# Local attention's weighted sums added up by accumulating DMAs, and a second fold on GpSimd, in a gated mix of two attentions

## Chip, core and metric

One core of a Trainium2 chip runs the kernel in one launch. The metric is the device time of one execution in microseconds (us); lower is better. TensorE is called PE below, VectorE DVE, ScalarE ACT, GpSimd Pool, and SyncE, which issues most DMAs, SP.

## What is computed

The input x has 2048 rows of 448 numbers. Two attention blocks of 16 heads of 28 numbers read it, and a gate mixes their results:

```
g = sigmoid((x * gate_w).sum(-1))
a = local attention A: q, k, v = x @ wqkv;  row s sees rows s, s-2, ..., s-14 (8 offsets w, step 2)
      logits[s, w] = q[s] . k[s - 2w] * 28**-0.5;  softmax over w;  o[s] = sum over w of p[s, w] * v[s - 2w];  o @ wo
b = full attention B: every row sees all 2048 rows;  o @ wo
out = g * a + (1 - g) * b
```

Everything is float32; products that need the precision are split into a high and a low part and summed from three matmuls.

## The kernel before

The kernel has three stages. Until about 254 us PE projects x to q, k and v of both blocks. From there until about 829 us it computes the full attention B, and beside it the local attention A, which uses no PE at all. From there to the end it multiplies both results by the output weights.

**The middle stage** has 256 steps: 16 units (four groups of heads by four blocks of 512 columns) of 16 steps each. A step is one pass of the loop `for kt in range(NJ)`. In it PE makes the scores of four heads (line 960), three matmuls of an early pass that looks for the maximum scores of a later unit (line 142), and the weighted sum of the step before (line 926). ACT takes the exponentials (line 965, two of 128x1024 per step), DVE the maxima (line 148). When a unit's maxima are complete, `max_parts` reduces them (line 176), ACT negates them, Pool makes their low part (line 183), DVE transposes them (line 188), and SP stores them to DRAM (`nm`, line 193) and loads them again as two more rows of the queries (`QH<-nm`). PE's first scores of the next unit wait for that load.

**The local attention** is cut into 8 chunks c of two heads each. Rows lie over 128 partitions, 16 rows to a partition, so that one tile is 128x896 (16 rows, 56 numbers). For each chunk and each offset w:

- `a_score`: Pool multiplies q by the shifted k (line 604, 128x896), and folds the 28 products of a head to 14 by adding one half to the other (line 609, 128x448).
- `a_reduce`: DVE sums what is left to one logit per row and head (line 614). `NR[c, w]` says in how many pieces, and `a_score` folds `3 - NR` times: with 2 once, with 1 twice.
- `a_softmax`: nine small steps on Pool, DVE and ACT (lines 616 to 644).
- `a_av`: Pool multiplies v by the weight of this offset (line 654, part 0), into `oat` for w = 0 and into a tile `prod2` for the others, and then adds `prod2` to `oat` (line 659, part 1). `prod2` and the products of `a_score` share one tag of five buffers.

After the last addition of a chunk SP stores `oat` to DRAM (`oa_scr`, line 662). When all chunks are done, `a_done` frees their buffers and sets the loads for the last stage (`op_load_b`, `op_load_a`).

**Order.** Every engine runs its instructions in the order in which the program issues them, and a waiting instruction holds up all behind it on its engine. For the local attention that order comes from a planner at build time: `item` enters each piece with a key, a cost in us and the pieces it needs, each with a lag in steps; `issue` puts a piece into the running step if its needs were issued early enough and the cost still fits (for Pool up to 4.2 us of backlog, worn down by 2.1 or 2.2 us per step). The costs are constants in the code; at run time the engines follow the order that came out of them, and the semaphores.

Of the kernel before, what the change touches and what calls it, by code (L numbers as in the profile page):

```python
# [11 lines left out]
ALU = mybir.AluOpType  # L12
# [13 lines left out]
def gated_mix_kernel(ctx: ExitStack, tc: tile.TileContext, xT, xn, gw, wA, wB, woAB, out):  # L26
    nc = tc.nc
# [180 lines left out]
    with tc.tile_pool(name="xp", bufs=1) as xp, tc.tile_pool(name="wp", bufs=2) as wp:  # L208
# [208 lines left out]
        for kt in range(3):  # L417
            if kt < 2:
                nc.vector.tensor_copy(xh[0][:, kt, :], r[:, kt, :])
            nc.vector.tensor_tensor(out=xl[0][:, kt, :], in0=r[:, kt, :], in1=xh[0][:, kt, :].bitcast(F32),  # L420
                                    op=ALU.subtract)
        nc.vector.tensor_tensor(out=tail[64:128], in0=t[64:128], in1=tail[64:128].bitcast(F32), op=ALU.subtract)
        nc.vector.tensor_tensor(out=wl0[:, 3, 0:256], in0=wt0[:, 0:256], in1=wh0[:, 3, 0:256].bitcast(F32),
                                op=ALU.subtract)
# [27 lines left out]
        for n, t in enumerate(tiles):  # L452
# [48 lines left out]
            if n == 64:  # L501
                gate = []
                for sgn, dst in ((-1.0, g_t), (1.0, omg)):
                    e = sp.tile([128, NJ], F32, name="ez")
# [14 lines left out]
    def at(pos, st, f):  # L519
        hooks.setdefault((st, pos), []).append(f)  # L520
# [10 lines left out]
    pool = ctx.enter_context(tc.tile_pool(name="psv", bufs=1, space=bass.MemoryType.PSUM))  # L531
# [56 lines left out]
    qt, Lt, oat, lst, prods = {}, {}, {}, {}, {}  # L588

    def a_load(c, nme):  # L590
        if nme == "q":
            qt[c] = a2.tile([128, NJ, 56], F32, name="qt")
            nc.sync.dma_start(qt[c], a_own[0][c])
        else:
            t = kvt[nme, c % 2]
            i = 1 if nme == "k" else 2
            nc.sync.dma_start(t[:, 0:HALO, :], a_prev[i][c, :, NJ - HALO:NJ, :])
            nc.sync.dma_start(t[:, HALO:, :], a_own[i][c])

    def a_score(c, w):  # L600
        if w == 0:
            Lt[c] = a2.tile([128, W, NJ, 2], F32, name="L", bufs=3)
        p = a3.tile([128, NJ, 56], F32, tag="prod", name="prod")
        nc.gpsimd.tensor_tensor(out=p, in0=qt[c], in1=kvt["k", c % 2][:, HALO - DIL * w:HALO - DIL * w + NJ, :],  # L604
                                op=ALU.mult)
        prods[c, w] = p.rearrange("p j (h d) -> p (j h) d", d=DH)
        for n in (DH // 2, DH // 4)[:3 - NR[c, w]]:
            lo, hi = prods[c, w][:, :, 0:n], prods[c, w][:, :, n:2 * n]
            nc.gpsimd.tensor_tensor(out=lo, in0=lo, in1=hi, op=ALU.add)  # L609
            prods[c, w] = lo  # L610

    def a_reduce(c, w, i, n):
        r = slice(2 * NJ // n * i, 2 * NJ // n * (i + 1))
        nc.vector.tensor_reduce(Lt[c][:, w].rearrange("p j h -> p (j h)")[:, r], prods[c, w][:, r], axis=X, op=ALU.add)

    def a_softmax(c, i):
        L = Lt[c].rearrange("p w j h -> p w (j h)")
        Lw = Lt[c].rearrange("p w j h -> p (j h) w")
        if i == 0:
            nc.gpsimd.tensor_tensor(out=L, in0=L, in1=maskt.rearrange("p w j h -> p w (j h)"), op=ALU.add)  # L620
        elif i in (1, 2):
            if i == 1:
                lst["m"] = a2.tile([128, NJ * 2], F32, name="lm")
            r = slice(NJ * (i - 1), NJ * i)
            nc.vector.tensor_reduce(lst["m"][:, r], Lw[:, r], axis=X, op=ALU.max)
        elif i == 3:
            nc.gpsimd.tensor_tensor(out=L, in0=L, in1=lst["m"][:, None, :].to_broadcast([128, W, NJ * 2]),
                                    op=ALU.subtract)
        elif i == 4:
            nc.scalar.activation(L, L, AF.Exp, scale=SCALE)  # L630
        elif i in (5, 6):
            if i == 5:
                lst["z"] = a2.tile([128, NJ * 2], F32, name="ls")
            r = slice(NJ * (i - 5), NJ * (i - 4))
            nc.vector.tensor_reduce(lst["z"][:, r], Lw[:, r], axis=X, op=ALU.add)
        elif i == 7:
            r = a2.tile([128, NJ, 2], F32, name="lr")
            nc.vector.reciprocal(r.rearrange("p j h -> p (j h)"), lst["z"])
            lst["r"] = r
        else:  # L640
            r = lst["r"]
            nc.gpsimd.tensor_tensor(out=r, in0=r, in1=g_t[:, :, None].to_broadcast([128, NJ, 2]), op=ALU.mult)
            nc.gpsimd.tensor_tensor(out=L, in0=L, in1=r.rearrange("p j h -> p (j h)")[:, None, :].to_broadcast(
                [128, W, NJ * 2]), op=ALU.mult)

    def a_av(c, w, part):
        if part == 0:
            if w == 0:
                oat[c] = a2.tile([128, NJ, 56], F32, name="oat")
                dst = oat[c]  # L650
            else:
                dst = a3.tile([128, NJ, 56], F32, tag="prod", name="prod2")
            oat[c, w] = dst
            nc.gpsimd.tensor_tensor(  # L654
                out=dst.rearrange("p j (h d) -> p j h d", d=DH),
                in0=kvt["v", c % 2][:, HALO - DIL * w:HALO - DIL * w + NJ, :].rearrange("p j (h d) -> p j h d", d=DH),
                in1=Lt[c][:, w, :, :, None].to_broadcast([128, NJ, 2, DH]), op=ALU.mult)
        else:
            nc.gpsimd.tensor_tensor(out=oat[c], in0=oat[c], in1=oat[c, w], op=ALU.add)  # L659
            if w == W - 1:  # L660
                stored[0] = now[0] + 4
                at("end", stored[0], lambda: nc.sync.dma_start(oa_scr[:, :, 56 * c:56 * c + 56], oat[c]))


# [3 lines left out]
    now = [0]  # L668
    stored = [0]

    def item(eng, key, name, cost, needs, f):
        lists[eng].append((key, name, cost, needs, f))

    CH, NR = 21, {}
    for c in range(8):
        for w in range(W):
            NR[c, w] = 2
    last = lambda c, w: ("r", c, w, NR[c, w] - 1)
    for c in range(8):
        c0 = CH * c - 5 * (c == 7)  # L680
        for nme in "qkv":
            item("sp", c0 if nme != "v" else c0 + 18, ("ld", nme, c), 0,
                 [(("s", c - 2, 7), 3)] if nme != "v" else [(("a", c - 2, 7, 1), 3)],
                 lambda c=c, nme=nme: a_load(c, nme))
        for w, o in enumerate((0, 2, 5, 8, 11, 14, 17, 20)):
            back = (c, w - 4) if w > 3 else (c - 1, w + 4)
            item("pool", c0 + o, ("s", c, w), 3.15 + 0.5 * (NR[c, w] == 1),
                 [(("ld", "k", c), 4), (("ld", "q", c), 4), (("a", c - 3, 7, 0), 0), (("s", c, w - 1), 0)]
                 + ([(last(*back), 0)] if back in NR else []), lambda c=c, w=w: a_score(c, w))
            for i in range(NR[c, w]):  # L690
                item("dve", c0 + o + 2 + 0.1 * i, ("r", c, w, i), 0.32,
                     [(("s", c, w), 3), (("r", c, w, i - 1) if i else last(c, w - 1) if w else ("r",), 0)],
                     lambda c=c, w=w, i=i: a_reduce(c, w, i, NR[c, w]))
        for i, (eng, o, cost, lag) in enumerate((("pool", 22, 0.68, 2), ("dve", 23, 0.35, 3), ("dve", 23.5, 0.35, 0),
                                                 ("pool", 25, 0.68, 1), ("act", 26, 0.3, 3), ("dve", 27, 0.35, 1),
                                                 ("dve", 27.5, 0.35, 0), ("dve", 27.8, 0.36, 0),
                                                 ("pool", 28, 0.9, 1))):
            item(eng, c0 + o, ("m", c, i), cost, [(last(c, 7) if i == 0 else ("m", c, i - 1), lag)],
                 lambda c=c, i=i: a_softmax(c, i))
        n = 0  # L700
        for w in range(W):
            for part in ((0,) if w == 0 else (0, 1)):
                item("pool", CH * c + 30 + 1.4 * n, ("a", c, w, part), 1.65 if part == 0 else 2.05,
                     [(("m", c, 8), 0), (("ld", "v", c), 4),
                      (("a", c, w - 1, 1 if w > 1 else 0) if part == 0 else ("a", c, w, 0), 0)],
                     lambda c=c, w=w, part=part: a_av(c, w, part))
                n += 1
    for q in lists.values():
# [350 lines left out]
```

## Time and profile before

| | before |
|---|---|
| median of 3 runs | 911.59 us (911.21 to 912.66) |
| the profiled execution | 911.58 us, span of its instructions 909.8 us |
| TensorE clock granted | 1.0 throughout |
| PE busy | 901.1 us, 99% of the span |
| DVE, ACT, Pool busy | 731.8, 649.3, 640.0 us |
| DMA | 105.06 MB, 115 GB/s on average |

The profile comes from one execution. Its 1.78 us beside the span are the start and the end around the first and last instruction. Matmuls overlap, so that PE's share says little of how near it is to its limit. `L659` in a row is line 659 of the kernel before.

### The profile page before, as it was taken

To read this page: it belongs to the slowest core of one execution; us is meant where nothing else is said; L and a number is where in the kernel's file an instruction comes from. 1 tells how busy PE (TensorE), PEld (TensorE's weight loads), DVE (VectorE), ACT (ScalarE), POOL (GpSimd) and SP (SyncE) were. 2 spreads that over 40 slices of the span, in tenths; PEclk is the share of its full clock that TensorE was granted. 3 is DMA by queue.
4 is the path that set the end of the run, shared out by engine and by line. 5 is a ranking of instruction groups with operands and counts; after the bars stand their busy time and mean duration, and the time that the engine had idled before them with its cause. 6 is when DMAs were issued, how large, how long until landed. Compare 5 with 4: busy or idle time off the path is not lost.

```text
span 909.8 us, 20654 instructions
## 1 busy us (share of the span) xinstructions
PE 901.1 (99%) x8390; PEld 547.1 (60%) x8390; DVE 731.8 (80%) x934; ACT 649.3 (71%) x797; POOL 640.0 (70%) x505
## 2 busy tenths in 40 slices
PE   9999999999999999999999999999999999999998
PEld 6799999999954444444444444444444444336887
DVE  5588999999979999999999999999999988411221
ACT  6456434343378898898988898988989888995211
POOL 2389846564468659999999999999999987710100
PEclk9999999999999999999999999999999999999999
DMA  9877503459462341235235315421411321353672
GB/s 267 281 249 195 160 12 83 133 138 108 114 244 65 103 121 45 59 87 135 57 83 143 88 45 143 101 94 40 106 34 34 95 54 41 101 165 94 211 206 85
DMA packets 103960, 105.06 MB, mean 115 GB/s; under 512 B 64136, under 2 KB 73736, under 8 KB 103080
## 3 DMA queue, kind: packets, MB, share of 16 engines
q1 hardware_dynamic: 103720, 103.47, 41.4%
q8 instruction: 66, 1.08, 0.5%
q10 hardware_dynamic: 144, 0.26, 0.1%
q14 instruction: 30, 0.25, 0.1%
HBM read 62.72 MB, written 40.96 MB: 114 GB/s over the span
## 4 chain that ended last, share of the span: by engine, by line
PE 95%; DMA 2%; ACT 2%; DVE 1%; issue 0%; SPq 0%; ACTq 0%; DVEq 0%
PE T L960 29%; PE av L926 27%; PE r L300 15%; PE r L295 7%; PE T L809 6%; PE T L142 5%; PE r L142 4%; DMA oal<-oa_scr 1%; ACT P L965 1%; PE T L787 1%; DMA V<-in_xT 1%; DMA KH<-qk_hi 0%; ACT KH L748 0%; DVE res L818 0%; DVE xl L420 0%
## 5 line engine op out<-in xcount | busy, mean ns | idle before, releaser
L965 ACT ACTIVATE P<-T 128x1024 f32<-128x1024 f32 x512 | 496.9, 1025 | 57.4 <-PE T L960 56.1
L148 DVE TENSOR_REDUCE MX<-T 128x1 f32<-128x512 f32 x470 | 448.4, 957 | 32.1 <-PE T L142 13.1
L926 PE MATMUL av<-P,V 128*32 128x512 f32 x2048 | 272.7, 605 | 0.9 <-ACT osb L827 0.9
L960 PEld LDWEIGHTS T<-QH,KH 30*128 30x128 f32 x1024 | 92.7, 181 | 228.9 <-ACT P L965 197.8
L142 PE MATMUL T<-KH,QP 28*128 28x512 f32 x704 | 221.4, 460 | 0.1
L960 PE MATMUL T<-QH,KH 30*128 30x512 f32 x1024 | 212.0, 489 | 0.5 <-DMA QH<-nm 0.5
L164 DVE TENSOR_REDUCE MX<-r 128x2 f32<-128x1024 f32 x160 | 191.7, 1222 | 25.6 <-PE r L142 24.3
L960 PE MATMUL T<-QH,KL 28*128 28x512 f32 x1024 | 186.7, 394 | 0.0
L960 PE MATMUL T<-QL,KH 28*128 28x512 f32 x1024 | 185.4, 393 | 0.0
L604 POOL TENSOR_TENSOR prod<-qt,kt 128x896 f32<-128x896 f32 x64 | 135.3, 2114 | 7.9 <-DMA kt<-a_scr 4.5
L363 ACT ACTIVATE raw<-r 128x896 f32<-128x896 f32 (+1 forms) x64 | 58.9, 921 | 97.1 <-PE r L300 94.8
L659 POOL TENSOR_TENSOR oat<-oat,prod 128x896 f32<-128x896 f32 x56 | 118.1, 2109 | 2.7
L142 PEld LDWEIGHTS T<-KH,QP 28*128 28x128 f32 x704 | 86.0, 181 | 30.3 <-ACT P L965 22.0
L364 POOL TENSOR_TENSOR ast<-raw 128x448 f32<-128x448 f32 x48 | 55.3, 1153 | 58.1 <-ACT raw L363 49.2
L654 POOL TENSOR_TENSOR prod<-vt,L 128x896 f32<-128x896 f32 x56 | 95.4, 1704 | 0.4
L960 PEld LDWEIGHTS T<-QH,KL 28*128 28x128 f32 x1024 | 93.5, 183 | 0.7
L960 PEld LDWEIGHTS T<-QL,KH 28*128 28x128 f32 x1024 | 93.6, 184 | 0.0
L926 PEld LDWEIGHTS av<-P,V 128*32 128x32 f32 x2048 | 40.3, 108 | 76.4 <-issue 63.4
L300 PE MATMUL r<-wh,xh 64*128 64x448 f32 (+1 forms) x512 | 83.2, 363 | 0.0
L142 PE MATMUL r<-KH,QP 64*128 64x512 f32 x320 | 80.3, 392 | 1.0 <-DMA KH<-qk_hi 0.6
L300 PE MATMUL r<-wh,xl 64*128 64x448 f32 (+1 forms) x384 | 70.7, 364 | 0.0
L609 POOL TENSOR_TENSOR prod<-prod 128x448 f32<-128x448 f32 x64 | 65.5, 1023 | 5.0
(109 smaller groups left out, 1074.3 us busy)
## 6 DMA issues: line engine op xcount, KB each, us to landing
a_scr<-ast SPq DMA_DIRECT2D x24, 448.0 KB
qk_hi<-qkh SPq DMA_DIRECT2D x24, 256.0 KB
qk_lo<-qkh SPq DMA_DIRECT2D x24, 256.0 KB
rbc<-rs SPq DMA_DIRECT2D x64, 64.0 KB
QP<-qk_hi SPq DMA_DIRECT2D x64, 56.0 KB
KL<-qk_lo SPq DMA_DIRECT2D x16, 224.0 KB
QH<-qk_hi SPq DMA_DIRECT2D x64, 56.0 KB
QL<-qk_lo SPq DMA_DIRECT2D x64, 56.0 KB
```

What stands on the lines that cost most here:

```text
L142: nc.tensor.matmul(bank, qhis[u][h % 2][r, 128 * qs:128 * qs + 128], KH[u // NB % 3][r, 512 * kc:512 * kc + 512], start=True, stop=True)
L148: i = nc.vector.tensor_reduce(MX[:, n % NMX:n % NMX + k], bank, axis=X, op=ALU.max)
L164: nc.vector.tensor_reduce(m, PM[k], axis=X, op=ALU.max)
L295: nc.tensor.matmul(bank, ws[c][rows, k, t[4]:t[4] + 128], x, start=first, stop=last)
L300: nc.tensor.matmul(bank[:, 0:cols], x, ws[c][rows, k, 0:cols], start=first, stop=last)
L604: nc.gpsimd.tensor_tensor(out=p, in0=qt[c], in1=kvt["k", c % 2][:, HALO - DIL * w:HALO - DIL * w + NJ, :], op=ALU.mult)
L609: nc.gpsimd.tensor_tensor(out=lo, in0=lo, in1=hi, op=ALU.add)
L654: nc.gpsimd.tensor_tensor(out=dst.rearrange("p j (h d) -> p j h d", d=DH), in0=kvt["v", c % 2][:, HALO - DIL * w:HALO - DIL * w + NJ, :].r ...
L659: nc.gpsimd.tensor_tensor(out=oat[c], in0=oat[c], in1=oat[c, w], op=ALU.add)
L926: nc.tensor.matmul(av[32 * h:32 * h + 32, :], V[:, kt, 4 * g + h, :], tiles_[h], start=(kt == 0), stop=(kt == NJ - 1), skip_group_check=True)
L960: nc.tensor.matmul(bank[a], (KH[g % 3], KH[g % 3], KL[g % 2])[t][r, ks], (qh, ql, qh)[t][r, :], start=(t == 0), stop=(t == 2))
L965: e = nc.scalar.activation(p, one if a == "2" else mine, AF.Exp, scale=SCALE).ins
```

## The change

The addition of `prod2` to `oat` is no longer an instruction on Pool but a DMA that adds to its destination (`accum_op`), issued from Pool's queue. Pool folds every product a second time (14 to 7 numbers per head), since `NR` is 1 everywhere, and DVE sums each in one piece instead of two. The planner's entries follow: another cost for both parts, and a need of two steps between two additions to the same `oat`; the store of a chunk is placed five steps after its last addition is issued instead of four.

```diff
@@ a_av
         else:
-            nc.gpsimd.tensor_tensor(out=oat[c], in0=oat[c], in1=oat[c, w], op=ALU.add)
+            nc.gpsimd.dma_start(out=oat[c].rearrange("p j e -> p (j e)"), in_=oat[c, w].rearrange("p j e -> p (j e)"),
+                                accum_op=ALU.add)
             if w == W - 1:
-                stored[0] = now[0] + 4
+                stored[0] = now[0] + 5
                 at("end", stored[0], lambda: nc.sync.dma_start(oa_scr[:, :, 56 * c:56 * c + 56], oat[c]))
@@ the planner's entries
         for w in range(W):
-            NR[c, w] = 2
+            NR[c, w] = 1
...
-                item("pool", CH * c + 30 + 1.4 * n, ("a", c, w, part), 1.65 if part == 0 else 2.05,
+                item("pool", CH * c + 30 + 1.4 * n, ("a", c, w, part), 1.7 if part == 0 else 1.1,
                      [(("m", c, 8), 0), (("ld", "v", c), 4),
-                      (("a", c, w - 1, 1 if w > 1 else 0) if part == 0 else ("a", c, w, 0), 0)],
+                      (("a", c, w - 1, 1 if w > 1 else 0) if part == 0 else ("a", c, w, 0), 0)]
+                     + ([(("a", c, w - 1, 1), 2)] if part and w > 1 else []),
                      lambda c=c, w=w, part=part: a_av(c, w, part))
```

## The prediction

> **What bounds the kernel now.** I read the page first, then the groups by form, then windows of one unit each, and last the timeline around the end of the middle stage.
>
> ```profile
> PE 901.1 (99%) x8390; PEld 547.1 (60%) x8390; DVE 731.8 (80%) x934; ACT 649.3 (71%) x797; POOL 640.0 (70%) x505
> PE 95%; DMA 2%; ACT 2%; DVE 1%; issue 0%; SPq 0%; ACTq 0%; DVEq 0%
> ```
>
> The chain of waits is 95% PE: Pool is nowhere on it and DVE has 1%. The change takes work from Pool and DVE alone, so the question is whether either one holds PE up in a place that an average hides. Three units of 16 steps, as windows (us, then busy us of PE, PEld, DVE, ACT, POOL, clock, DMA share), and the same windows for line 614 alone:
>
> ```profile
> 651.16:687.12 35.96, 35.96 (x374) 14.93 (x372) 33.84 (x46) 32.01 (x36) 33.89 (x22) 1.00 0.15 42
> 723.06:759.01 35.95, 35.95 (x374) 15.06 (x372) 32.76 (x43) 32.30 (x38) 27.45 (x20) 1.00 0.21 49
> ...
> 363.65:399.57 35.92, 2.58 (x7) 1.00 0.29 79
> 651.16:687.12 35.96, 4.14 (x11) 1.00 0.15 42
> 723.06:759.01 35.95, 0.75 (x2) 1.00 0.21 49
> ```
>
> The first two rows are the whole core, the last three line 614 alone. Units with 7, 11 and 2 of DVE's local sums last 35.92, 35.96 and 35.95 us. Pool busy falls from 33.89 to 27.45 and nothing moves either. So the unit's 35.95 us (2.247 per step) is a loop of PE, ACT and the maxima; neither the local sums nor Pool's load set it.
>
> **What is removed and added on Pool and DVE.**
>
> ```profile
> L604 POOL TENSOR_TENSOR prod<-qt,kt 128x896 f32<-128x896 f32 x64 | 135.3, 2114 | 7.9 <-DMA kt<-a_scr 4.5 <-DVE L L614 3.4
> L659 POOL TENSOR_TENSOR oat<-oat,prod 128x896 f32<-128x896 f32 x56 | 118.1, 2109 | 2.7
> L654 POOL TENSOR_TENSOR prod<-vt,L 128x896 f32<-128x896 f32 x56 | 95.4, 1704 | 0.4
> L609 POOL TENSOR_TENSOR prod<-prod 128x448 f32<-128x448 f32 x64 | 65.5, 1023 | 5.0
> L614 DVE TENSOR_REDUCE L<-prod 128x16 f32<-128x224 f32 x128 | 47.6, 372 | 0.0
> L642 POOL TENSOR_TENSOR lr<-lr,g_t 128x32 f32<-128x32 f32 x8 | 2.0, 245 | 16.2 <-DVE lr L638 8.8 <-ACT P L965 7.4
> L593 SPq DMA_DIRECT2D qt<-a_scr x8: 337/379/552, 257.2 to 606.0; - x8
> q1 hardware_dynamic: 103720, 103.47, 41.4%
> ```
>
> Pool loses 56 additions: 118.1 us. It gains 64 folds of 224 numbers; between L642 (32 numbers, 0.245 us) and L609 (448, 1.023 us) a straight line gives 0.60 us each, 38.7 us. It gains 56 issues of an accumulating DMA, which no row shows. Below it lies SP's issue of a transfer of the same 448 KB (0.38 us, L593), above it the addition it replaces (2.11 us). I take 1.1 us: a Pool instruction of its own, priced between the small and the mid-sized rows. Break-even is (118.1 - 38.7)/56 = 1.42 us per transfer, waiting included; at 1.1 us Pool is freed of 18 us, at 2.1 it is loaded by 39.
>
> DVE loses 64 of 128 sums. The one that stays reads the same 224 numbers (32 groups of 7 for 16 of 14), so 0.37 us stands and 64 x 0.372 = 23.8 us go. By the windows that is worth 0 on the path. Its cover is the PE loop; DVE's idle time before L614 is 0.0, so it has never waited for a fold, and the second fold's 0.6 us per product stays hidden as long as Pool keeps its place.
>
> **The added wait.** Each accumulation must wait for the landing of the one before it on the same `oat`, and it waits in Pool's queue: behind it stand later products and folds, `fin_on`, and the low part of the maxima (L183), for which DVE, then SP, then PE wait. So the figure that decides is the time L from issue to landing.
>
> ```profile
> 773.88 0.35 SPq L845 DMA_DIRECT2D rs<-finv  x1
> 775.31 2.26 SPq L850 DMA_DIRECT2D rbc<-rs  x4
> 859.06 5.17 DMA oal<-oa_scr
> ```
>
> The smallest round trip I find is 8 KB: `rbc` reads what `rs<-finv` writes and is issued 775.31 - 773.88 = 1.43 us after it, of which 0.35 is issue, 1.08 the rest. Queue q1 moved 103.47 MB in 41.4% of the span, 376.7 us: 275 GB/s while busy, so 448 KB (0.459 MB) take 1.67 us once, 3.34 if the destination is read as well as the source. So L lies between 0.38 + 1.08 + 1.67 = 3.1 us and, in a busy stretch, where 224 KB took 5.17 us (the chain's row at 859.06), 5.17 + 1.67 + 1.7 = 8.5. I take 1.1 + 1.1 + 2.5 (between one pass and two) = 4.7 alone, and with a fifth of the transfer time given to others (DMA share 0.15 to 0.29) the 2.5 becomes 3.1: L = 5.3 us.
>
> The Trainium skill, Collectives: The Full Stack, section on why ReduceScatter is half of AllGather, says that an adding transfer is slower because of its two source reads, not because of the addition. DMA: Bandwidth & Descriptors, section on the anatomy of a SWDGE DMA, fits 2.0 us plus bytes over 436 GB/s. An estimate from both is 2.0 + 2 x 1.05 = 4.1 us, and by it no accumulation here would wait; that is rival 1. No row of this trace shows such a transfer.
>
> In the planned order two accumulations of a chunk stand at least 2 steps (4.49 us) apart. Of 48 such gaps 33 have 3 steps or more (6.7 us), and L = 5.3 hides in them. Nine of 2 steps lie in chunks 0, 2, 4 and 6: 9 x 0.8 = 7 us of waiting, spread over units in which Pool now has 18 us less to do. I count 0.2 us for that. The six of chunk 7 follow one another directly, and they end where the trace has no cover:
>
> ```profile
> 757.52 1.70 POOL L654 TENSOR_TENSOR oat<-vt,L 128x896 f32<-128x896 f32 x1
> ...
> 763.02 1.29 POOL L864 TENSOR_TENSOR onlo<-on,onhi 128x512 fp32r<-128x512 f32 x1
> ...
> 783.56 1.28 POOL L856 TENSOR_TENSOR on<-osb,rbc 128x512 f32<-128x512 f32 x1
> 784.80 0.22 POOL L183 TENSOR_TENSOR nmt<-nmv,nmt 128x16 fp32r<-128x16 f32 x1
> 785.06 0.21 DVE L188 STREAM_TRANSPOSE nms<-nmt 128x32 f32<-128x32 f32 x1 [2.32 <-POOL nmt L183]
> 785.30 1.72 SPq L193 DMA_DIRECT2D nm<-nms  x4
> 791.38 1.06 SPq L99 DMA_DIRECT2D QH<-nm  x2
> 793.83 0.43 PEld L960 LDWEIGHTS T<-QH,KH 30*128 30x128 f32 x4 [1.40 <-DMA QH<-nm]
> 795.96 0.19 PEld L960 LDWEIGHTS T<-QH,KH 30*128 30x128 f32 x4 [0.84 <-issue]
> ```
>
> These rows are one path: Pool's L183, DVE's transpose, SP's store of the maxima, its loads in order, and PE's first weights of the last unit, which wait 1.40 us where the next step waits 0.84. So 0.56 us is exposed already, and each us by which L183 slips comes out whole. In the changed order from 757.52 on Pool does two products (1.70 us each) and `fin_lo` (L864, 1.29), 4.7 us, issues the first accumulation at 762.2, and L183 follows the fifth and one product: 762.2 + 4L + 1.1 + 1.7 = 765.0 + 4L. Between them stand 2.8 to 4.1 us of other Pool work, less than L, so L sets the pace. At L = 4.95 L183 stands at 784.8 as before; at 5.3 it comes 1.4 us later; a smaller L can win the 0.56 us at most.
>
> Right behind it the sixth accumulation moves twice 448 KB (3.3 us of all transfer engines) while SP stores the maxima and loads the queries: 0 to 1.7 us of collision, one pass at most; I take 0.8, about the middle.
>
> **What is moved.** By the planner's list the local part ends at step 244, not 241, so that the loads of the last stage stand three steps later in SP's queue, past `rbc` of the last but one unit.
>
> ```profile
> 812.27 0.84 SPq L768 DMA_DIRECT2D oal<-oa_scr  x2
> 825.67 0.66 PE L787 MATMUL T<-ident,oal 128*128 128x128 f32 x4
> ```
>
> From issue to need there are 13.4 us; three steps (6.7) and the slowest landing of such a load seen (5.17) leave 1.5. I cost it at nothing; if the cover goes, the last stage starts later by what is missing.
>
> **The sum** against the profiled execution's 911.58 us (the median of the runs is 911.59, so nothing is to be converted): 0 for DVE, + 0.2 for the gaps in the middle, + 1.4 for L183, + 0.8 for the collision = + 2.4: **914.0 us**. With L from 4.7 to 5.8 the L183 term runs from -0.6 to + 3.4 and the collision from 0 to 1.7, so this case's own range is 911 to 917. 0.2% (1.8 us) is about what a measurement of this kernel can tell from no change.
>
> **Rivals.**
>
> 1. *The accumulations land in time* (L under 4.9). Then no wait is added: the gain is the exposed 0.56 us, the cost a part of the collision: 911.4, within 0.2%. For it: the lower bound of 3.1 us. Against it: the doubled reads, and 5.17 us for half the bytes in a busy stretch.
> 2. *Pool becomes the bound.* Its point is L over 6 us, or over 1.42 us of Pool per accumulation. At L = 7 L183 stands at 793.0, + 8.2; the nine short gaps cost 9 x 2.5 = 22 us of Pool, of which the 18 us freed cover most, + 4, and the products of offsets behind them reach DVE late; with the collision 926. At 2.1 us per issue alone 39 us are added to a queue with 35.96 - 33.89 = 2.1 us free per unit, 29 over 14 units: + 10 to + 39, up to 950. For it: Pool is nearly full, and an order fixed at build does not give. Against it: gaps of 3 steps are the rule.
> 3. *DVE's relief shortens steps: faster.* DVE is busy 33.84 of 35.96 us, 0.13 us idle per step, and a sum of 0.372 overflows that by 0.24. If one in five of the 64 removed sums stands where DVE ends last, 13 x 0.24 = 3.1 us go: 908.5. Against it: the windows with 2 and 11 sums are equally long.
>
> **The numbers.** The forecast gets 0.50, of which 0.15 lies within 0.2% and 0.35 above; rival 1 0.14; rival 2 0.17; rival 3 0.19. So faster 0.19, same 0.29, slower 0.52. The range 908 to 930 leaves out the larger half of rival 2 and the far end of rival 3.
>
> **What the profile after would show.** Right: units 1 to 13 still 35.95 us; Pool's busy sum near 560; accumulations of chunk 7 about 5.3 us apart with Pool idle between; PE's wait on `QH<-nm` at the last unit near 3.5 us. Wrong: L183 late at an earlier unit, or DVE's line 614 waiting for Pool (rival 2); units under 35.7 us (rival 3).

## The result and the profile after

The changed kernel takes **927.85 us** (median of 4 runs, 926.57 to 929.03). The kernel before, run beside it, takes 911.75 (911.21 to 912.66). The ratio is 1.0175, 95% interval 1.0155 to 1.0196: 16 us slower, where 2.4 were forecast.

From the page of the changed kernel (busy time, DMA queues with packets, MB and share, chain of waits by engine):

```profile
PE 905.4 (98%) x8390; PEld 548.0 (59%) x8390; DVE 718.1 (78%) x870; ACT 650.2 (70%) x797; POOL 618.9 (67%) x569
...
q1 hardware_dynamic: 103720, 103.47, 40.7%
q0 software_dynamic: 8064, 25.69, 15.3%
...
PE 64%; POOL 18%; DMA 11%; issue 3%; SPq 2%; DVE 1%; ACT 0%; POOLq 0%; ACTq 0%
```

Every compute engine has about the same or less to do, and yet Pool, which had no visible share of the chain before, and DMA, which had 2%, now hold 29% of it. Queue q0 is new: the accumulating transfers. Its groups by form (the first two of Pool's, the last of DVE's):

```profile
L659 POOL DMA_DIRECT2D oat<-prod x56 | 49.0, 874 | 45.9 <-DMA oat<-prod 38.3 <-POOL prod L654 5.1 <-DMA rbc<-rs 2.3
L609 POOL TENSOR_TENSOR prod<-prod 128x224 f32<-128x224 f32 x64 | 45.4, 709 | 5.0
...
L614 DVE TENSOR_REDUCE L<-prod 128x32 f32<-128x224 f32 x64 | 23.9, 373 | 0.0
```

And the last line of the view of line 659, the time from issue to landing:

```profile
DMA to landing us min/median/max: 4.2/5.0/8.9
```

For the 118.1 us of additions Pool now has 49.0 us of issues, 5.1 us of standing until the product just made is complete, and 45.4 us of second folds. It is freed of 118.1 - 49.0 - 5.1 - 45.4 = 18.6 us, and then stands 38.3 us for landings. The rows of its products have grown as well (line 604 from 135.3 to 145.3 us, line 654 from 95.4 to 103.7), but an instruction behind a transfer is shown to begin before the issue ends (one at 774.60, where the issue runs from 773.99 for 0.88 us), so these rows overlap. By the page's busy sums the relief is 640.0 - 618.9 - 5.1 = 16.0 us.

Where the time went, by windows of one unit each (lines past 704 are numbered 2 higher than before, so the exponentials are line 967). The columns are those of the windows shown above:

```profile
400.37:436.26 35.89, 35.89 (x374) 14.99 (x372) 32.38 (x40) 31.85 (x34) 33.00 (x29) 1.00 0.67 160
544.76:583.33 38.57, 36.01 (x374) 14.91 (x368) 33.53 (x45) 32.24 (x36) 34.14 (x30) 1.00 0.76 171
583.33:624.25 40.92, 38.20 (x372) 15.54 (x372) 32.10 (x41) 32.07 (x37) 34.73 (x32) 0.96 0.57 127
...
768.44:809.68 41.24, 35.88 (x353) 14.44 (x349) 24.81 (x28) 33.13 (x39) 24.51 (x21) 0.96 0.61 132
```

An undisturbed unit (the first row; it is unit 4, counted from 0) lasts 35.9 us as before. Three units make most of the loss: 8 (+ 2.6), 9 (+ 5.0) and 14 (+ 5.4; it had 35.85 before). Four others lose 0.2 to 0.5 us each, the last unit 0.8. From the first exponential to the end of the last, the middle stage grew from 573.7 to 588.7 us: + 15.0.

**Unit 8** starts with a collision. SP's issues (start, us, what):

```profile
543.57 0.35 SPq L593 DMA_DIRECT2D qt<-a_scr  x1
543.98 0.41 SPq L597 DMA_DIRECT2D kt<-a_scr  x1
544.44 0.42 SPq L598 DMA_DIRECT2D kt<-a_scr  x1
```

Pool's timeline over the same stretch, and ACT's at its end (in brackets the idle time before, and what ended it):

```profile
544.39 0.86 POOL L659 DMA_DIRECT2D oat<-prod  x1
...
553.36 1.70 POOL L654 TENSOR_TENSOR prod<-vt,L 128x896 f32<-128x896 f32 x1 [2.67 <-DMA oat<-prod]
...
579.43 1.26 POOL L858 TENSOR_TENSOR on<-osb,rbc 128x512 f32<-128x512 f32 x1
```
```profile
580.73 0.63 ACT L862 ACTIVATE onhi<-on 128x512 fp32r<-128x512 f32 x1 [2.60 <-POOL on L858]
```

And the window from that transfer's issue to its landing:

```profile
544.40:553.30 8.90, 8.90 (x96) 3.67 (x92) 8.22 (x11) 8.32 (x12) 6.13 (x7) 1.00 0.92 227
```

The accumulation goes out among three loads of the next chunk (DMA share 0.92), and its landing takes 8.9 us. The next product waits 2.67 us for a tile that the transfer still holds. From there Pool works with hardly a gap, and 26 us later it starts `on` (L858) late. ACT stands 2.60 us for it (its `onhi`, L862), with the exponentials behind, and PE behind those.

**Unit 9** is the same by another door: a landing of 5.9 us behind a gap of two steps, 3.84 us of waiting, and L183 late for DVE.

```profile
596.68 0.88 POOL L659 DMA_DIRECT2D oat<-prod  x1 [3.84 <-DMA oat<-prod]
603.45 0.21 DVE L188 STREAM_TRANSPOSE nms<-nmt 128x32 f32<-128x32 f32 x1 [2.83 <-POOL nmt L183]
```

DVE's maxima stand behind that transpose, and PE behind the maxima. PE was then busy for 1.63 of 3.41 us, and for the next 3.41 us its granted clock (third column from the right) was 0.50:

```profile
601.94:605.35 3.41, 1.63 (x13) 0.37 (x5) 1.90 (x4) 1.40 (x2) 3.33 (x6) 1.00 0.18 34
605.35:608.76 3.41, 3.34 (x18) 1.04 (x18) 2.13 (x4) 1.94 (x2) 3.33 (x3) 0.50 0.66 116
```

**Unit 14** is the place that the prediction named. Pool in chunk 7:

```profile
773.99 0.88 POOL L659 DMA_DIRECT2D oat<-prod  x1 [0.30 <-POOL prod L654]
...
779.69 0.88 POOL L659 DMA_DIRECT2D oat<-prod  x1 [3.09 <-DMA oat<-prod]
...
784.49 0.88 POOL L659 DMA_DIRECT2D oat<-prod  x1 [2.01 <-DMA oat<-prod]
...
790.25 0.88 POOL L659 DMA_DIRECT2D oat<-prod  x1 [3.16 <-DMA oat<-prod]
...
795.63 0.88 POOL L659 DMA_DIRECT2D oat<-prod  x1 [1.53 <-DMA oat<-prod]
...
797.90 0.52 POOL L183 TENSOR_TENSOR nmt<-nmv,nmt 128x16 fp32r<-128x16 f32 x1
```

The chain from there (start, us, what), after SP's loads in order:

```profile
805.40 0.50 SPq L99
805.95 1.92 DMA QH<-nm
808.00 1.77 PE T L962 x12
809.77 1.87 PE av L928 x8
```

PE's first matmuls after it, with the idle time before them, and windows around PE's return:

```profile
808.00 0.92 PE L962 MATMUL T<-QH,KH 30*128 30x512 f32 x4 [5.36 <-DMA QH<-nm]
```
```profile
803.32:806.73 3.41, 0.00 (x0) 0.00 (x0) 2.15 (x2) 0.96 (x2) 1.42 (x2) 1.00 0.80 189
806.73:813.56 6.83, 5.56 (x36) 2.33 (x40) 0.62 (x1) 3.19 (x5) 0.58 (x1) 0.50 0.87 229
813.56:816.97 3.41, 3.41 (x37) 1.15 (x31) 0.63 (x1) 3.41 (x5) 0.00 (x0) 1.00 0.19 44
```

The transfers stand (795.63 - 773.99) / 4 = 5.4 us apart with Pool idle between them. L183 follows the fifth, then SP's stores and loads, then PE. PE has stood still for 5.36 us. Its granted clock fell to 0.50 before it came back and stayed there until 813.56: eight `av` matmuls take 1.87 us where a later step takes 1.0. The stall is paid a second time.

### The profile page after: what moved, and what is told of

The parts are those of the page before. It is cut to its first block, busy times and chain, and to the rows that moved or that the text cites. A ratio compares the mean times of both kernels' runs of the same rounds, so it can differ in the third digit from the quotient of the medians.

```text
span 924.8 us, 20717 instructions
## 1 busy us (share of the span) xinstructions
PE 905.4 (98%) x8390; PEld 548.0 (59%) x8390; DVE 718.1 (78%) x870; ACT 650.2 (70%) x797; POOL 618.9 (67%) x569
## 3 DMA queue, kind: packets, MB, share of 16 engines
q0 software_dynamic: 8064, 25.69, 15.3%
## 4 chain that ended last, share of the span: by engine, by line
PE 64%; POOL 18%; DMA 11%; issue 3%; SPq 2%; DVE 1%; ACT 0%; POOLq 0%; ACTq 0%
PE r L300 15%; PE T L962 15%; PE av L928 14%; DMA oat<-prod 7%; PE r L295 7%; PE T L811 6%; POOL prod L604 5%; PE r L142 4%; POOL prod L654 4%; POOL prod L609 4%; PE T L142 2%; POOL oat L659 2%; DMA kt<-a_scr 1%; SPq L99 1%; POOL oat L654 1%
## 5 line engine op out<-in xcount | busy, mean ns | idle before, releaser
L604 POOL TENSOR_TENSOR prod<-qt,kt 128x896 f32<-128x896 f32 x64 | 145.3, 2270 | 5.1 <-DMA kt<-a_scr 5.1
L609 POOL TENSOR_TENSOR prod<-prod 128x448 f32<-128x448 f32 (+1 forms) x128 | 110.9, 866 | 10.0
L654 POOL TENSOR_TENSOR prod<-vt,L 128x896 f32<-128x896 f32 x56 | 103.7, 1852 | 2.7 <-DMA oat<-prod 2.7
L659 POOL DMA_DIRECT2D oat<-prod x56 | 49.0, 874 | 45.9 <-DMA oat<-prod 38.3
```

Of the source, the lines that this page charges most:

```text
L654: nc.gpsimd.tensor_tensor(out=dst.rearrange("p j (h d) -> p j h d", d=DH), in0=kvt["v", c % 2][:, HALO - DIL * w:HALO - DIL * w + NJ, :].r ...
L659: nc.gpsimd.dma_start(out=oat[c].rearrange("p j e -> p (j e)"), in_=oat[c, w].rearrange("p j e -> p (j e)"), accum_op=ALU.add)
```

## Experiments

Theory at the start: Pool waits in its own queue for each landing, and the second fold has used up the room in which it could catch up; chunk 7's chain costs some 6 us by itself. Rivals: the second fold alone; traffic that slows other loads; DVE's relief worth something. Each kernel was timed against the kernel before on the same chip. "Stage" is the middle stage of the profiled run, from the start of the first exponential to the end of the last, worked out from the trace; it leaves out the start, which lay between 255.5 and 259.0 us in these profiles.

| kernel | median us | ratio to before (95%) | landing, median us | transfers' waits us | stage us |
|---|---|---|---|---|---|
| before | 911.75 | | | | 573.7 |
| changed | 927.85 | 1.0175 (1.0155 to 1.0196) | 5.0 | 38.3 | 588.7 |
| acc_alone | 927.12 | 1.0177 (1.0161 to 1.0193) | 4.8 | 43.2 | 588.0 |
| fold_alone | 944.63 | 1.0368 (1.0352 to 1.0384) | | | 608.0 |
| c7_pool | 921.31 | 1.0105 (1.0092 to 1.0119) | 4.9 | 21.5 | 583.7 |
| only_c7 | 921.98 | 1.0095 (1.0080 to 1.0109) | 4.8 | 15.3 | 582.7 |
| acc_quarter | 911.99 | 1.0007 (0.9998 to 1.0016) | 3.0 | 7.4 | 574.7 |
| acc_half | 914.79 | 1.0026 (1.0018 to 1.0034) | 3.4 | 17.6 | 575.8 |
| plain_copy | 912.47 | 0.9996 (0.9988 to 1.0005) | 3.3 | 14.5 | 573.9 |
| quarter_bulk | 914.53 | 1.0022 (1.0010 to 1.0035) | 3.3 | 21.1 | 575.0 |
| no_chain | 918.52 | 1.0071 (1.0050 to 1.0091) | 5.0 | 0 | 575.7 |
| no_chain_six_tiles | 921.34 | 1.0102 (1.0083 to 1.0120) | 5.0 | 0 | 580.6 |
| spaced_c7 | 946.63 | 1.0375 (1.0360 to 1.0391) | 4.8 | 17.1 | 606.7 |
| late_products | 917.08 | 1.0053 (1.0040 to 1.0066) | 4.8 | 9.9 | 576.9 |

### The two parts by themselves

`acc_alone`, the transfers without the second fold, with the changed kernel's prices and lags in the planner:

```diff
-            NR[c, w] = 1
+            NR[c, w] = 2
-  3.15 + 0.5 * (NR[c, w] == 1)
+  3.65
```

> The 56 accumulating transfers with the changed kernel's plan (the planner's prices and lags of the changed kernel), but one fold per score and two DVE sums again: Pool loses the 64 second folds, 45.4 us. Theory (the second fold's 45 us use up what the transfers free, so Pool is late in the middle and the 38 us of waits for landings then reach ACT and DVE; chunk 7's chain costs some 6 us by itself): the 8.6 us of units 6 to 13 go, the last unit's 6 us stay: 918 (916 to 920), first exponential to last 6 us longer than before, waits of the accumulations for landings shorter than 38 us and not on the chain of waits before unit 14. Rival 1 (the transfers alone cost it all, by their waits or their traffic): 926 to 929. Rival 2 (the second fold alone costs it): 911 to 913.

927.12: without the second fold's 45 us on Pool, and with DVE's 24 back, the time is the same. My theory missed here, and the first rival held: the transfers by themselves cost as much. The sum is the same, its places are not: DVE has two sums per product again, so the planner's order comes out a little different, and here units 2, 8 and 14 lose 4.4, 1.6 and 6.8 us, and unit 9 nothing. That the fold makes no difference at all is therefore not shown, only that taking it away brings nothing back. Taking 45 us of work from a queue that waits for landings leaves longer waits (43.2 instead of 38.3 us), and more of them at the tiles (who waited, for what: us in total, times, longest):

```profile
POOL oat L659 <- DMA oat<-prod: 43.2, 20, 4.0
POOL prod L654 <- DMA oat<-prod: 8.9, 2, 7.6
```

`fold_alone`, the second fold with the additions on Pool, at the planner's prices of before, so that the planner does not know of the second fold:

```diff
-            NR[c, w] = 2
+            NR[c, w] = 1
-  3.15 + 0.5 * (NR[c, w] == 1)
+  3.15
```

> The second fold and the one-piece DVE sum alone, with the additions on Pool and the plan of the kernel before (the planner is not told of the second fold): Pool gains 45 us over before, DVE loses 24. Theory (Pool has little room to spare in the stage with the local part; 45 us more on it are more than the changed kernel's net load of about 33 us): slower than before by at least the 8.6 us that the changed kernel lost in its middle, 924 (919 to 934), with the losses in units in the middle where ACT waits for Pool's products and DVE for Pool's maxima, and nothing special at the last unit. Rival 1 (only the transfers cost): 911 to 913, units of 35.95 us. Rival 3 (DVE's relief is worth something): below 911.

944.63, over twice the loss expected. In this order Pool has no room for 45 us more, and the waits for it show where it ends:

```profile
ACT onhi L860 <- POOL on L856: 21.6, 10, 4.4
```

So the second fold costs 33 us on top of the additions, where leaving it out beside the transfers, which free Pool, brings nothing. By the planner's list the local part ends at step 236 here and at 241 before, so a part of the 33 us may be the denser order; a plan that prices the fold was not run.

### How long a landing takes

`acc_quarter` and `acc_half` accumulate 224 and 448 of each partition's 896 numbers; `plain_copy` copies all 896 and does not add.

```diff
-  out=oat[c]..., in_=oat[c, w]..., accum_op=ALU.add
+  out=oat[c]...[:, 0:224], in_=oat[c, w]...[:, 0:224], accum_op=ALU.add     # acc_quarter; 0:448 in acc_half
+  out=oat[c]..., in_=oat[c, w]...                                          # plain_copy
```

> The changed kernel with the same plan and the same order, but each of the 56 transfers accumulates only the first 224 of 896 elements of each partition (three quarters of the addition are left out): Pool's issue stays, the landing gets shorter. Theory (waits for landings cost, not the issue): landing falls from 5.0 us to about 3 (2.5 to 4), the waits of the accumulations from 38 us to under 15, chunk 7's pitch to 4 us or less, the last step of unit 14 to under 4.5 us and the long units 8 and 9 lose at least half of their excess: 917 (914 to 920). Rival 1 (Pool's own time, issue and second fold, is what is too much; the wait only shows it): 924 to 928. Rival 2 (the traffic's four-fold volume on the DMA rings slows other loads): also near 915, but with the landings of the K loads and QH shorter as well.

> The changed kernel, but each transfer accumulates 448 of 896 elements of each partition (half of the addition is left out). Between the quarter's landing (3.0 us) and the whole's (5.0) a straight line gives 3.7 us. Theory A: waits of the accumulations of 10 to 20 us, chunk 7's pitch near 4.2 us, 914.5 (912 to 918). If there is a point from which the landings collide (Pool's slack used up only beyond it), it is near 912, like the quarter.

> The changed kernel, but each transfer copies the product over the sum and does not add (seven products are left out): the same chain, the same writes, and no reading of the target. If the reading of the target takes part in the landing time (the Trainium skill, Collectives: The Full Stack, has an adding transfer read two sources), the landing falls from 5.0 us to about 4 and theory A gives waits of about 22 us and 919 (914 to 924). If the addition costs nothing at the landing: 5.0 us again and 926 to 929.

The quarter takes 911.99, the kernel before within its interval, with every instruction on Pool and DVE in its place, the second fold included. So it is the transfer's size that costs, by its landing or by its traffic, and not the work on Pool and DVE. From `acc_quarter` the landing of line 659, and the window of unit 14:

```profile
DMA to landing us min/median/max: 2.6/3.0/7.8
```
```profile
761.34:797.11 35.77, 35.77 (x359) 14.28 (x361) 21.97 (x27) 33.00 (x40) 24.82 (x21) 1.00 0.45 102
```

From `plain_copy` the view of line 659 (ns of the issue, then us to landing), and queue q0 of its page:

```profile
L659 POOL DMA_DIRECT2D oat<-prod x56: 577/577/722, 343.0 to 794.2; - x56
...
DMA to landing us min/median/max: 2.7/3.3/7.7
```
```profile
q0 software_dynamic: 4480, 25.69, 7.5%
```

The plain copy of the whole product costs nothing (0.9996), which I had given at 914 or more. With the same bytes counted, the addition takes 8064 packets for 4480, 15.3% of the DMA engines' time for 7.5%, 0.88 us of Pool's issue for 0.58, and 5.0 us to land for 3.3. At 3.3 us ten transfers still wait, 14.5 us in all, but the stage is as long as before (573.9 and 573.7). Half an accumulation, at 3.4 us and 17.6 us of waiting, costs 2.4, most of it in units 8, 9 and 14 (+ 0.2, + 0.8, + 0.7): the median landing does not tell these two apart, and which of the differences between them does is not shown.

### The chain, the traffic and the tiles

`no_chain`: each transfer adds the product's tile onto that tile itself and not onto the running sum, so that none waits for the one before.

```diff
-  out=oat[c]..., in_=oat[c, w]..., accum_op=ALU.add
+  out=oat[c, w]..., in_=oat[c, w]..., accum_op=ALU.add
```

> The changed kernel with the same plan, order, issues and bytes, but each transfer adds its product tile onto that tile itself and not onto the running sum: no transfer has to wait for the one before (the running sum then lacks seven of the eight products). Theory A (the chain: Pool's queue stands at each transfer until the one before has landed): the waits of the accumulations for landings, 38 us, go, landings stay near 5.0 us, chunk 7's pitch falls to about 4 us or less, the last step of unit 14 to under 3 us, no long units: 912 (911 to 914). Theory B (the traffic: 448 KB each way slow the loads that others wait for, and the chain is not what costs): 921 to 928. If both count, the middle units keep some of their 8.6 us: 914 to 920.

918.52, with the landings at 5.0 us still. Of 16 us the chain makes 9 to 10; 6 stay, so the chain and something else both hold a part. The runs lie far apart (914.98 to 922.63), and the profiled one is the fastest; its stage is only 2.0 us longer than before. Over a whole run the clock was granted at 0.999 to 1.0 in the three shortest (up to 917.76) and at 0.993 to 0.996 in the three longest (from 919.28), so what stays goes together with a clock that falls as in units 9 and 14; no trace of the longer runs was kept. `no_chain_six_tiles` asked whether the rest is the tiles that a transfer holds until it lands:

```diff
-  tile_pool(name="a3", bufs=5)     oat: bufs=2, stored 5 steps after the last transfer
+  tile_pool(name="a3", bufs=6)     oat: bufs=1, stored 3 steps after the second product
```

> The run without the chain (each transfer adds its product onto itself, seven of eight products left out of the sum), with six tiles for products instead of five; the sum's tile is single and stored after the second product, to make room. That run lay at 918.5, 6 us above the kernel before, with its runs 915 to 923. If the rest is the taking of the tiles until the landing: 911 to 914 with a narrow spread. If it is the traffic at the other loads: 916 to 920, with the same spread.

Six tiles brought nothing back: 921.34. In the profile of `no_chain` the products wait for a tile for 0.3 us in all, which also speaks against the tiles; but the room for the sixth cost the second `oat` and moved the store, so this run by itself does not exclude them. Its profile shows one way in which traffic costs, from the chain of waits at unit 14:

```profile
778.36 3.73 SPq L853
...
783.81 3.87 DMA rbc<-rs
...
792.96 5.04 DMA nm<-nms
```

One issue on SP takes 3.73 us (median of these 64: 0.42), `on` and with it L183 wait for `rbc`, and the maxima then need 5.04 us to land. This run stored a chunk just ahead of that issue, where `no_chain` did not, so it does not prove the same for the other.

`quarter_bulk` brings traffic back without a wait on it:

```diff
   (acc_quarter)
+  at("end", now[0], lambda: nc.sync.dma_start(bulk[7 * c + w - 1], V[:, 0:2]...))     # 512 KB to DRAM
```

> The run with a quarter of each transfer (912.0), plus, for each of the 56 transfers, a copy of 512 KB from a tile that no longer changes to a place in DRAM that nobody reads, issued from SP's queue at the end of the same step. The copies bring back about the ring time that the three quarters took (8 to 10 points of share), without a wait in Pool's queue on them; SP issues 56 DMAs more of some 0.4 us. Chain alone (the traffic is harmless): 912 to 914. Traffic alone (it slows the loads and the transfers, as the 6 us that stayed without the chain suggest): 916 to 920, with longer landings of the quarter transfers (above 3.5 us in the median) and longer landings of the maxima and of rbc. Traffic makes up the whole: 924 or more.

914.53: 1.0022 times before where the quarter alone has 1.0007, 1.4 us. The hardware queue's share rises from 41.8 to 50.5%, the landing of the transfers from 3.0 to 3.3 us, and their waits from 7.4 to 21.1 us:

```profile
POOL oat L660 <- DMA oat<-prod: 21.1, 13, 3.3
```

The result lies between what was expected of the chain alone and of traffic alone: this traffic is worth one to two us, in part through the landings again. What else makes up the 6 us of `no_chain` stays open.

### Chunk 7, and other orders

`c7_pool` gives chunk 7's additions back to Pool, `only_c7` takes the kernel before and gives only chunk 7's to transfers.

```diff
+            if c == 7:      # only_c7: if c != 7
+                nc.gpsimd.tensor_tensor(out=oat[c], in0=oat[c], in1=oat[c, w], op=ALU.add)
+            else:
                 nc.gpsimd.dma_start(... accum_op=ALU.add)
```

> The changed kernel, but the seven additions of chunk 7 by Pool's tensor_tensor again, planned at 2.05 us each. Theory (seven serial landings of about 5.4 us in chunk 7 hold up Pool's store of the maxima for the last unit): pitch from product to product of chunk 7 falls from 5.4 to about 4 us, the last step of unit 14 falls from 7.8 us to 3 to 4, total 922 (920 to 924), units 8 and 9 stay long. Rival (the last unit is late because the plan starts chunk 7's products one step later, or because of traffic at the loads, whatever adds): 926 to 929.

> The kernel before, with chunk 7's seven additions alone by accumulating transfers (one fold, two DVE sums, the plan of before up to chunk 7's products, which start at step 223 as before and not 224). Theory (the chain of seven landings of 5 us delays the last unit's maxima by itself): pitch of chunk 7's transfers 5.0 to 5.4 us, the last step of unit 14 at 4 to 6.5 us instead of 2.3, all other units 35.95: 915 (913.5 to 917). If the one step later in the plan was what made it: 911 to 913.

`c7_pool` gains 6.5 us, as expected, and its unit 14 is back at 35.85 us. `only_c7` loses 9 us where 3.5 were expected, and all in one unit (windows of units 13 and 14):

```profile
725.37:761.32 35.95, 35.95 (x374) 14.95 (x372) 32.68 (x43) 32.27 (x38) 27.50 (x20) 1.00 0.22 49
761.32:805.97 44.65, 37.37 (x355) 14.95 (x353) 24.10 (x28) 33.43 (x40) 22.72 (x20) 0.91 0.62 134
```

Pool in that unit, the first and the sixth transfer:

```profile
763.52 1.03 POOL L660 DMA_DIRECT2D oat<-prod  x1 [0.32 <-POOL prod L654]
...
792.13 0.88 POOL L660 DMA_DIRECT2D oat<-prod  x1 [2.75 <-DMA oat<-prod]
...
794.40 0.52 POOL L183 TENSOR_TENSOR nmt<-nmv,nmt 128x16 fp32r<-128x16 f32 x1
```

In this order L183 stands behind the sixth transfer of the chunk and not the fifth: five landings, (792.13 - 763.52) / 5 = 5.7 us each. And the clock falls: 0.91 over the unit. So a single chain of transfers in front of one wait that PE feels is enough for a loss of about 9 us.

Two kernels space the transfers of chunks 0 to 6 at least three steps apart, with chunk 7 on Pool. `spaced_c7` (one fold) delays the transfer, `late_products` (two folds) the product:

```diff
+  [(("a", c, w - 1, 1), 3)] if part and w > 1 and c < 7          # spaced_c7, planned at 1.25 us
+  [(("a", c, w - 1, 1), 3)] if part == 0 and w > 1 and c < 7     # late_products
```

> One fold and two DVE sums as before; chunks 0 to 6 add by transfers, planned at 1.25 us and at least three steps apart (two in the changed kernel), chunk 7 adds on Pool. The full traffic of 49 transfers of 448 KB stays, the waits for landings should fall under 10 us. Theory A: 912 to 914, all units 35.9 to 36.5 us. Theory B: 918 to 922 as with chunk 7 on Pool alone. That this beats the kernel before would need Pool's relief to be worth something: the undisturbed units of all runs say it is not.

> Second fold as in the changed kernel; chunk 7 adds on Pool; in chunks 0 to 6 each product is planned three steps or more after the transfer before it was issued (in the changed kernel it is planned at once and its transfer waits). So no transfer comes sooner than three steps after the one before, as in the run with spaced transfers, but a product lies in its tile for no or one step before its transfer (there up to three). Theory (a landing of 5 us costs through two doors: the next transfer waits for it, and the product's tile, one of five, stays taken until then; traffic itself costs little): waits for landings under 10 us at transfers and under 10 us at products, units of 36 us, 913 to 916. Rival (49 landings of 448 KB slow the other loads, whatever the order): 919 to 924. Rival (spacing itself ruins the plan, as the 946.6 us of the spaced transfers might say): over 930.

`spaced_c7` is the slowest of all, 946.63. Its waits:

```profile
POOL prod L654 <- DMA oat<-prod: 30.0, 10, 3.8
POOL prod L604 <- DMA oat<-prod: 22.7, 10, 5.5
POOL oat L662 <- DMA oat<-prod: 17.1, 9, 2.9
```

The waits of the transfers fell from 38.3 to 17.1 us, and 52.7 us appeared at the products: in 21 of 49 cases a product now lies three steps in its tile before its transfer is even issued, and with five tiles the next product or score finds none. The two kernels differ in more than the spacing: in the fold, which speaks the other way, and in how dense the order is (by the planner's list the local part ends at step 231 in `spaced_c7`, at 246 in `late_products`), so that spacing alone made the 946.63 is not shown. With the product late instead, only one line is left:

```profile
POOL oat L662 <- DMA oat<-prod: 9.9, 6, 2.4
```

917.08: of the changed kernel's excess about a third stays. `c7_pool` differs from it only in the order of chunks 0 to 6, where nine gaps between transfers are two steps long and here none is; that is worth 1.0105 - 1.0053, some 5 us. The waits do not add up to the loss: 9.9 us of them come with 5 us here, 14.5 in `plain_copy` with none. No version beats the kernel before, and nothing here says that one could: its units are at 35.95 us already.

## Why the prediction was right or wrong

**Direction and range: right, the size not.** Slower was the likeliest, and 927.85 lies in 908 to 930, but near its end. The forecast of 914.0 was 14 us too low, and the working's own range of 911 to 917 does not reach the result: the wide one does because its upper part was left to rival 2.

**The relief of DVE and Pool worth 0 on the path: right.** `acc_quarter` and `plain_copy` have DVE's 24 us less and land at 1.0007 and 0.9996. Rival 3 is out.

**Pool's balance: right by two errors that cancel.** The fold measured 0.709 us (taken: 0.60, 6.7 us too little in all), a transfer 49.0 + 5.1 us over 56 = 0.97 (taken: 1.1). 18.6 us freed, 18 forecast. The busy sum near 560 was a wrong mark: the page counts the issues as busy, so 618.9.

**The landing L: near, and in part by luck.** 5.3 taken, 5.0 measured; bounds 3.1 to 8.5, measured 4.2 to 8.9. The first four landings of chunk 7 took 5.2, 4.3, 5.2 and 4.8 us, 4.9 on average, which is where rival 1 began. But Pool issued the next transfer only 0.53 us after each landing (795.10 to 795.63 at the fifth), a term that the working left out, and so they stood 5.4 us apart, near the 5.3 taken for L alone. The estimate from the Trainium skill, DMA: Bandwidth & Descriptors, anatomy of a SWDGE DMA, with the source read twice, was 4.1 us; the trace has 5.0, and its fastest 4.2. The two source reads of the Trainium skill, Collectives: The Full Stack, why ReduceScatter is half of AllGather, agree with the runs: the addition doubled the share of the DMA engines' time, 15.3 against 7.5%.

**The gaps in the middle at + 0.2: the step that failed, about 9 us** (the stage's 15.0 less 5.4 and 0.8 in the last two units). The waits were too short: nine gaps at 0.8 us made 7 us, and the trace has 38.3 - 14.0 (chunk 7's six waits) = 24.3. Of these 18.7 stand at eight of the nine gaps of two steps, and 5.6 behind gaps of three, where the landing before took 7.5 to 8.7 us. Two steps of the plan were not 4.49 us on Pool: after one issue it came to the next 2.6 to 3.9 us later, like the 2.8 to 4.1 that the working had for chunk 7, whose transfers the planner also puts two steps apart.

The price was wrong as well: I set the waiting against 18 us of freed Pool, as if it were a load that could be spread. A queue that runs in order does not spread it: `on` and L183 stand behind. What a wait costs depends on what follows it. Unit 8 lost 2.6 us with one wait of 2.67 at a product's tile, unit 9 5.0 with one of 3.84, and unit 13 0.5 with three of 7.5 in all. `acc_alone` has 45 us more room and no less loss.

Rival 2 came nearest, with 926 at L = 7, and its signs are there: L183 was late in unit 9, and with 0.97 + 38.3 / 56 = 1.65 us per accumulation its point of 1.42 was passed. But its reason, that Pool is full, is not what `acc_alone` shows.

**L183 at + 1.4: mis-sized.** From the first transfer to L183 the working gave 2.8 + 4 x 5.3 = 24.0 us; the trace has 797.90 - 773.99 = 23.9. But the first transfer came 773.99 - 768.44 = 5.6 us after the unit's start and not 762.2 - 759.01 = 3.2: in the changed plan chunk 7's products start one step later, which I had not followed. L183 slipped by 29.5 - 25.8 = 3.7 us.

**The collision at + 0.8: right.** From L183 to PE's first matmul 808.00 - 797.90 = 10.1 us, before 793.86 - 784.80 = 9.1: + 1.0.

**What was missing: the clock after a stall.** Unit 14 lost 5.4 us, of which 3.7 + 1.0 are explained. 0.7 more, and 0.8 in the first step of the last unit, are left over, and they lie where the clock was 0.50: an estimate of 1.5 us on top of a delay of 4.7. In unit 9 PE was busy for 3.34 us at 0.50; half of that, an estimate of up to 1.7 us, is a part of its 5.0. The prediction costed each us of lateness at one us, and did not price the gate. The Trainium skill, TensorE: Matmul & The Clock Gate, part 1 on the HAM clock gate, has it: after an idle window of some 3.4 us the gate passes half the pulses, until PE has been busy for about as long. The trace agrees in unit 14, with 0.50 after 3.41 us without PE. In unit 9 it goes further: PE had been busy for 1.63 us of the 3.41 before the fall, so here no full idle window was needed.

**The last stage's loads at 0: right.** From the last exponential to the end of the span 80.0 us, before 80.6.

## What to carry to other kernels

A DMA that replaces an instruction is priced by its landing, and by what stands behind its wait in the queue and in the tiles it holds, not by the instruction that it saves: here the same plan cost nothing at 3.3 us and 16 us at 5.0. Steps of a plan are not time on an engine that runs ahead of them: count the work that the engine has between two issues. Waiting in an in-order queue can't be set against freed time; each wait must be placed in front of the instruction that it delays. To test such a change cheaply, shorten the transfer and leave everything else: if the time comes back, the load on the engines was not the question, and landing and traffic are left to be told apart.

## Hardware, not expected

- In the changed kernel an accumulating transfer of 448 KB between tiles takes 0.88 us of Pool's issue and lands after 4.2 to 8.9 us, 5.0 in the median; in `plain_copy` a plain one takes 0.58 and lands after 3.3. The addition makes 144 packets per transfer at each of the three sizes run, the plain copy 80.
- Pool issued a transfer that waited for a landing 0.53 us after that landing (795.10 to 795.63).
- After 3.41 us without PE its clock was granted at 0.50 for 6.83 us; after 3.41 us with PE busy for 1.63 it was 0.50 for 3.41 us.
- One DMA issue on SP took 3.73 us where 0.42 is the median, in a stretch with accumulating transfers and a store ahead of it (`no_chain_six_tiles`).
